# Windowed attention and a token-mixing layer on one core: q in one load per batch with its queries reordered, merged evacuations, cast-in-flight weights, a new order

## The chip, the core and the metric

The kernel runs on 1 core of one Trainium2 chip. The time is the device time of one execution in microseconds (us). The kernel before was run three times, and its median is compared with that of the changed kernel. Engines are called by the names of the profile: PE (TensorE matmul) with PEld (its weight loads), DVE (VectorE), ACT (ScalarE), POOL (GpSimd) and SP (SyncE, which issues stores).

## What is computed

Attention over 576 positions with a causal window of 128 and a distance bias, for 8 batches and 8 heads, and then a layer that mixes the tokens of a batch:

```python
scores = scale * np.matmul(q, k.transpose(0, 1, 3, 2))     # q, k, v: (8, 8, 576, 64)
mask = (rel >= 0) & (rel < 128)                            # rel = query - key
scores = np.where(mask, scores - slopes * abs(rel), -1e9)
attn = exp(scores - max) / sum
x = (attn @ v), heads side by side                         # (8, 576, 512)
wq, wk = x @ w_q, x @ w_k                                  # 512 -> 64
W_tok = (wq @ wk.T) / 8                                    # 576 x 576 for each batch
out = maximum(W_tok @ x, 0) @ w_out                        # float32
```

The kernel takes no maximum, and it evaluates W_tok @ x as wq @ (wk.T @ x): the product G = wk.T @ x is 64 x 512 for a batch.

## The kernel before

Tokens of a batch lie in four blocks of 128 and a tail of 64. Two batches form a pair, and the second layer works on pairs: a batch of a pair has half of the 64-row or 64-column tiles. All work is cut into named steps. `ORDER` (lines 39 to 116) lists every step with its engine (P, D, A, G, S) and, for TensorE, its PSUM bank; each engine runs its steps in this order, and semaphores do the waiting. `:P2` is a whole pair of banks (1024 fp32 columns), `:P21` one bank of pair 2. There are four pairs.

A batch `b` goes through these steps. `g` is a block of keys, `u` half of the heads.

- **Loads.** `Lq`, `Lk` and `Lv` (lines 358 to 381) are GpSimd DMAs that cast fp32 to f16 on the way: one for each block of 128 tokens, with 1024 pieces of 64 elements, and `Lt` for the tails of q and k of a pair. The first blocks of batch 0 come as fp32 through SP and ACT (`LF`). `Lw` and `Lwo` load the weights of the second layer as fp32 through SP, and VectorE casts them (`CWQ`, `CW`).
- **Transposes.** `TQ` (line 495) transposes q and k of one block with eight 128x128 transposes against the identity into one bank; `ETQ` copies the 1024 columns to `qkT`. `TT` and `ETT` do it for the tails, `TF`, `EF`, `TJ`, `EJ` for batch 0.
- **Scores.** `QK` (line 556) multiplies a block of keys with 256 queries, two heads at a time on the two row halves of the array, into a pair of banks. `EXP` (ScalarE) turns 1024 columns into f16 `pt`. `MUL` (VectorE) multiplies `pt` by `bias`, which holds exp of the distance bias and zeros outside the window; it runs once per `u`, and with `biasl` for the last block.
- **Values.** `PV` (line 601) multiplies `pt` by v with a column of ones; `RC` takes the reciprocals of the sums and `X` scales into `x`. `PV b.4` is the tail; it computes 128 rows, of which 64 are used.
- **Second layer.** `XT` and `XTT` transpose x, `EXT` and `EXTT` copy it out; `WQ`, `WK`, `WT` are the projections, `EWQ`, `EWK`, `EWT` their copies; `G` and `EG` make G; `MX` is wq @ G, transposed, in five parts, `RM` and `RMT` the relu to f16 (one instruction for each batch of the pair and each of four column groups, lines 792 to 805); `OUT` is the product with w_out for 128 rows, `EO` copies it to an fp32 buffer and `DO` stores it through SP.

`WM` steps are matmuls on zeros near the start. Two batches are in work at a time, and `OUT` steps of a pair are spread over the attention of the next one. The parameter `mode` says how a step tiles the array: 0 whole, 1 in two row halves, 2 in two column halves, 3 in both; it does not change what is emitted.

## Time and profile before

| | us |
|---|---|
| three runs: median (lowest, highest) | 140.9 (140.62, 145.1) |
| the profiled execution | 141.15 |
| its span | 139.3 |
| PE busy, 1846 matmuls | 125.9 (90%) |
| DVE busy, 254 instructions | 114.1 (82%) |
| ACT busy, 165 instructions | 112.2 (81%) |
| POOL busy, 118 instructions | 95.6 (69%) |
| exp, 64 on ACT, 1.033 each | 62.8 |
| output copies, 35 on ACT, 0.601 each | 20.7 |
| first exp starts, last exp ends | 10.52, 114.87 |
| last load issued on POOL, to landing some 5 later | 102.7 |
| packets of GpSimd's loads | 109,264 |

Busy times are unions over an engine's instructions. Matmuls are pipelined and their ends are modelled, so their duration (379 ns for 512 columns) is longer than the time from one start to the next. The mean granted TensorE clock is 0.987.

### The profile page before, as it was taken

What the parts mean: (1) busy time and instruction counts of PE and PEld (TensorE: products, weight loads), DVE (VectorE), ACT (ScalarE), POOL (GpSimd) and SP (SyncE); (2) the same over time, 40 slices, a digit from 0 to 9 for tenths busy, and PEclk for the clock granted to TensorE, in tenths of its full rate; (3) what the DMA queues carried; (4) which work ended last, traced back from release to release, by engine and by line L of the source; (5) the groups of instructions that cost most, each with busy time, mean ns of one, the idle gap of its engine ahead of it and who ended that gap; (6) DMA issues with size and microseconds to landing.
All of it is one profiled execution on the core that took longest, in us unless ns stands there. A gap on an engine that the chain in (4) does not pass through costs nothing.

```text
span 139.3 us, 4479 instructions
## 1 busy us (share of the span) xinstructions
PE 125.9 (90%) x1846; PEld 84.5 (61%) x1846; DVE 114.1 (82%) x254; ACT 112.2 (81%) x165; POOL 95.6 (69%) x118
## 2 busy tenths in 40 slices
PE   6778599879987999999999999999999999999970
PEld 4445486768744566767866477667765656754420
DVE  5657999999996999999999999999998999705000
ACT  3089969898796999868999999978989995279860
POOL 7999999999919999999999999759940000000000
PEclk9999869999999999999999999999999999999999
DMA  4999999999999999999999999999999975505993
GB/s 103 184 155 154 157 153 153 152 150 177 283 184 156 152 155 152 151 153 150 152 151 154 147 172 270 232 202 152 157 171 272 338 274 216 226 5 171 335 355 121
DMA packets 119332, 25.59 MB, mean 184 GB/s; under 512 B 114192, under 2 KB 114192, under 8 KB 119312
## 3 DMA queue, kind: packets, MB, share of 16 engines
q0 software_dynamic: 109264, 13.77, 155.9%
q1 hardware_dynamic: 8992, 11.28, 24.2%
q10 hardware_dynamic: 1056, 0.26, 0.8%
q8 instruction: 14, 0.23, 0.6%
q14 instruction: 6, 0.05, 0.1%
HBM read 29.62 MB, written 9.44 MB: 280 GB/s over the span
## 4 chain that ended last, share of the span: by engine, by line
PE 58%; POOL 22%; DMA 7%; DVE 7%; issue 2%; ACT 1%; ACTq 0%; POOLq 0%
PE pair L231 47%; POOL nat L363 13%; PE pair L234 11%; DMA natt<-in_k_dram 7%; POOL vt L380 6%; DVE pt L594 3%; DVE qkT L240 2%; POOL natt L370 2%; ACT osb L238 1%; DVE x L634 1%; DVE xT L240 0%; DVE rm L772 0%; POOL wm L298 0%; DVE xTt L240 0%; POOL wm L300 0%
## 5 line engine op out<-in xcount | busy, mean ns | idle before, releaser
L587 ACT ACTIVATE pt<-pair 128x1024 f16<-128x1024 f32 x64 | 62.8, 1033 | 4.0 <-PE pair L231 3.6
L380 POOL DMA_DIRECT2D vt<-in_v_dram x40 | 36.9, 976 | 2.6 <-PE pair L231 2.4
L363 POOL DMA_DIRECT2D nat<-in_k_dram x31 | 30.8, 1036 | 3.5 <-DMA nat<-in_k_dram 3.4
L231 PE MATMUL pair<-wout_sb,rm 128*128 128x512 f16 x128 | 31.6, 379 | 0.0
L594 DVE TENSOR_TENSOR pt<-pt,bias 128x1024 f16<-128x1024 f16 x48 | 31.3, 680 | 0.1
L363 POOL DMA_DIRECT2D nat<-in_q_dram x30 | 30.4, 1039 | 0.3 <-DMA vt<-in_v_dram 0.3
L238 ACT COPY osb<-pair 128x512 f32<-128x512 f32 x35 | 20.7, 601 | 7.4 <-PE pair L231 7.2
L231 PEld LDWEIGHTS <-pt 128*128 128x128 f16 x576 | 21.4, 98 | 8.4 <-issue 2.7
L231 PE MATMUL pair<-vt,pt 128*128 128x65 f16 x576 | 24.1, 195 | 2.3 <-ACT pt L587 1.6
L240 DVE COPY qkT<-pair 128x1024 f16<-128x1024 f16 (+1 forms) x38 | 21.7, 591 | 2.6 <-PE pair L231 1.3
L231 PE MATMUL pair<-qkT 64*128 64x256 f16 (+2 forms) x320 | 21.5, 250 | 1.1 <-DVE x L634 0.5
L634 DVE TENSOR_TENSOR x<-pair,inv 128x512 f16<-128x512 f32 x32 | 21.6, 685 | 0.5
L234 PE MATMUL pair<-identh,nat 128*128 128x128 f16 x244 | 19.3, 226 | 1.4 <-ACT pt L587 0.7
L234 PEld LDWEIGHTS <-nat 128*128 128x128 f16 x244 | 15.2, 101 | 5.8 <-issue 3.6
L231 PEld LDWEIGHTS <-rm 128*128 128x128 f16 x128 | 11.1, 97 | 10.6 <-issue 0.8
L231 PEld LDWEIGHTS <-qkT 64*128 64x128 f16 x320 | 11.3, 94 | 7.7 <-issue 3.2
L770 ACT ACTIVATE rm<-pair 128x512 f16<-128x512 f32 x25 | 13.7, 647 | 0.0
L594 DVE TENSOR_TENSOR pt<-pt,biasl 128x1024 f16<-128x1024 f16 x16 | 10.7, 668 | 0.0
L234 PE MATMUL pair<-identh,x 128*128 128x128 f16 x128 | 9.9, 219 | 0.0
L648 DVE RECIPROCAL inv<-pair 128x8 f32<-128x8 f32 (+1 forms) x40 | 7.8, 200 | 1.2 <-PE pair L231 0.8
L234 PEld LDWEIGHTS <-x 128*128 128x128 f16 x128 | 7.6, 98 | 1.7 <-issue 0.8
L240 DVE COPY xT<-pair 128x1024 f16<-128x1024 f16 x12 | 8.2, 687 | 0.4 <-PE pair L234 0.2
(66 smaller groups left out, 116.7 us busy)
## 6 DMA issues: line engine op xcount, KB each, us to landing
out_dram<-osb SPq DMA_DIRECT2D x32, 256.0 KB, 3.0
vt<-in_v_dram POOLq DMA_DIRECT2D x32, 128.0 KB, 5.5
nat<-in_k_dram POOLq DMA_DIRECT2D x31, 128.0 KB, 5.3
nat<-in_q_dram POOLq DMA_DIRECT2D x30, 128.0 KB, 5.1
osb<-in_moe_w_out_dram SPq DMA_DIRECT2D x4, 256.0 KB, 7.2
out_dram<-osb SPq DMA_DIRECT2D x8, 128.0 KB, 3.9
osb<-in_q_dram SPq DMA_DIRECT2D x4, 128.0 KB, 3.8
natt<-in_q_dram POOLq DMA_DIRECT2D x4, 128.0 KB, 7.1
```

Source lines behind the costliest of these rows:

```text
L231: hold(nc.tensor.matmul(*a, **k))
L234: hold(nc.tensor.transpose(*a))
L238: hold(nc.scalar.copy(out_ap, in_ap))
L240: hold(nc.vector.tensor_copy(out=out_ap, in_=in_ap))
L363: return lambda: nc.gpsimd.dma_start(out=natv(b, j, n), in_=(q, k)[j][b, :, P * n:P * n + P, :].transpose([1, 0, 2]))
L370: nc.gpsimd.dma_start(out=natt_s[pr % 2][:, j].rearrange("p e h d -> p (e h) d"), in_=(q, k)[j][2 * pr:2 * pr + 2, :, 512:576, :].rearrang ...
L380: return lambda: nc.gpsimd.dma_start(out=vtv(b, t)[:n, :, 0:D], in_=v[b, :, P * t:P * t + n, :].transpose([1, 0, 2]))
L587: nc.scalar.activation(out=pt[:, 0:1024], in_=two(s.bank).rearrange("p e c -> p (e c)"), func=AF.Exp, scale=SCALE)
L594: ENG2[o.eng].tensor_tensor(out=pt[:, 0:1024], in0=pt[:, 0:1024], in1=bt, op=ALU.mult)
L634: nc.vector.tensor_tensor(out=x[r].rearrange("p (g h d) -> p g h d", g=2, h=4), in0=sums(p)[r, :, :, 0:64], in1=box["inv"][r].unsqueeze(3) ...
L648: nc.vector.reciprocal(out=box["inv"][r], in_=sums(p)[r, :, :, 64])
L770: hold(nc.scalar.activation(out=out_ap, in_=in_ap, func=AF.Relu, scale=WSCALE))
```

## The change

- q of a whole batch (512 tokens) comes in one load: partition p gets the queries 4p to 4p+3, so a piece is 256 elements instead of 64. Batch 0 loads its second half like this. k keeps one load per block. The tails of q and k go to the two halves of the partitions.
- `TQ` transposes all of q in one step: 32 transposes of 128x64, in column halves. The queries of a block are thereby in another order: position 32r + x holds query 4x + r, in runs of 32. `iota` and `mask` build the bias in this order. x, wq and the mixed rows keep it, until `RM` writes its relu in the order r, x again; `OUT` st then computes the rows 4p + st, and `DO` stores them so.
- The new step `TK` transposes two blocks of k with sixteen pairs of 64x64 transposes in row halves (`tp2`), which write the two banks of a pair. `XT`, `XTT`, `TT` and the k of batch 0 (`TJ`) use `tp2` too and take two banks instead of one.
- `ETQ` copies 2048 columns; `QK` of a batch waits for it. `MUL` runs once for both `u`, 2048 columns, behind both `EXP`; `biasl` goes, the last block takes another slice of `bias`. `RM` does both batches of a pair, or two column groups, in one instruction of 1024 columns.
- The tail's `PV` does two groups of four heads in column halves, one bank, 64 rows each; `RC` and `X` of the tail have 128 partitions and half the columns, and `WT` and `G` take the tail in two halves.
- Weights are loaded by GpSimd with a cast, in four loads; `CWQ`, `CW`, `wz` go.
- The output step (7, 3) is done in two halves of 256 columns, each with its copy and store.
- `NPT` 5 to 6, `NNAT` 4 to 3 (k), `NQ` 2, `OSB` 12 to 14; other `WM` counts. The memsets of the pads of `pt` go.
- `ORDER` is new. At the start `ident` is behind six GpSimd items, and `bias` ahead of the first copies. 13 of 16 `RM` and 33 of 37 `EO` are on ScalarE, three `EO` and each one of `EWK`, `EWQ`, `EG` more than before on VectorE. `LOGB` and its steps are not used, since it is empty.

The diff, cut to what matters here (of the order, its start and its end):

```diff
-NNAT = 4
+NNAT = 3
+NQ = 2
+QR = 4
 NV = 4
-NPT = 5
-PTW = 1088
+NPT = 6
 NX = 4
 
 FIRST32 = ((0, 0), (1, 0), (0, 1))
 
-OSB = 12
-WIDE = ()
-
-WARM = (12, 3, 4, 3, 3, 5,)
+OSB = 14
+
+GROUPS = ((0, 1), (2, 3), (4, 5), (6, 7))
+
+LOGB = ()
+
+LAST = (7, 3)
+
+WARM = (25, 3, 2, 4,)
...
+warm:D LF0.0.1.0:A Lq0.2:G LF0.0.1.1:A LF0.1.0.0:S ones:D iota:G LF0.1.0.1:S LF0.0.0.1:S
+Lk0.1:G wmc:D zeros:D LF0.0.0.0:S mask:G Lk0.2:G bias:A Lq1.0:G ident:G Lk1.0:G idh:D WM.0:P31
+TF0.1.1:P00 pads:D TF0.0.1:P01 EF0.1.1:A Lk1.1:G TF0.1.0:P00 Lt0:G EF0.0.1:A TF0.0.0:P10
+EF0.1.0:A TJ0.1.1:P2 QK0.0.1:P3 EF0.0.0:D TJ0.2.1:P0 EXP0.0.1:A EJ0.1.1:D TJ0.2.0:P10 EJ0.2.1:D
...
+PV7.0:P2 OUT4.2:P11 RC7.2:D RC7.0:D X7.2:D OUT4.1:P00 EO4.2:A X7.0:D EO5.4:D XT7.1:P3 XTT6:P2
+OUT4.0:P11 EXT7.1:D EXTT6:A DO5.4:S EO4.1:A DO4.2:S OUT5.2:P10 DO2.1:S DO4.1:S XT6.1:P0 EO5.2:A
+XT7.0:P3 EXT6.1:D XT6.0:P2 EO4.0:A WT6:P10 EXT6.0:D EXT7.0:A OUT5.1:P11 EWT6:D WK6:P30 EO5.1:A
+DO5.1:S WQ6:P31 EWK6:A DO2.2:S DO3.2:S G6:P30 EWQ6:A DO4.0:S OUT5.3:P31 EG6:D MX6.0:P1 EO5.3:D
+MX6.4:P2 MX6.3:P0 RM6.0:A OUT4.3:P30 RMT6:D DO5.3:S DO2.3:S RM6.3:A MX6.1:P1 EO4.3:D MX6.2:P2
+DO5.2:S OUT7.4:P31 RM6.2:A RM6.1:D DO4.3:S OUT5.0:P30 EO7.4:A OUT7.2:P10 DO7.4:S EO5.0:A
+OUT6.1:P31 DO5.0:S EO7.2:A OUT7.1:P30 DO7.2:S EO6.1:A OUT7.0:P10 DO6.1:S EO7.1:A OUT6.2:P31
+DO7.1:S EO7.0:A OUT6.3:P30 DO7.0:S EO6.2:A OUT6.0:P10 DO6.2:S EO6.3:A OUT7.3b:P31 DO6.3:S
+EO6.0:A OUT7.3a:P30 DO6.0:S EO7.3a:A EO7.3b:A DO7.3a:S DO7.3b:S
...
+    bias = cpool.tile([P, 2, 2, 2, 384], F16, name="bias")
...
+    natq_s = [cpool.tile([P, H, QR, D], F16, name=f"natq{i}") for i in range(NQ)]
+    natk_s = [[cpool.tile([P, H, D], F16, name=f"natk{i}{n}") for n in range(4)] for i in range(NNAT)]
+    natt_s = [cpool.tile([P, 2, H, D], F16, name=f"natt{i}") for i in range(2)]
+    vt_s = [cpool.tile([P, 5, H, VW], F16, name=f"vt{i}") for i in range(NV)]
+    pt_s = [cpool.tile([P, 2, 1024], F16, name=f"pt{i}") for i in range(NPT)]
...
+    def twoh(bank):
+        return pairs[bank[0]].rearrange("p a c -> p (a c)").bitcast(F16).rearrange("p (a c) -> p a c", a=2)
...
+    def tp2(o, m, lo, hi):
+        for r, x in enumerate((lo, hi)):
+            k = slice(64 * r, 64 * r + 64)
+            tp(twoh(o.bank)[:, r, 64 * m:64 * m + 64], x[k], identh[k, k])
...
-        nc.gpsimd.iota(wint, pattern=[[1, 256]], base=0, channel_multiplier=-1)
+        nc.gpsimd.iota(wint[:, 0:256], pattern=[[P, 2], [1, QR], [QR, P // QR]], base=0, channel_multiplier=-1)
+        nc.gpsimd.iota(wint[:, 256:384], pattern=[[-P, 2], [1, 64]], base=P, channel_multiplier=-1)
...
+        keep(0, [[1, QR], [QR, P // QR]], 0, 1)
+        keep(P, [[1, QR], [QR, P // QR]], -1, -1)
+        keep(256, [[1, 64]], -1, -1)
+        keep(320, [[1, 64]], 0, 1)
...
+    def dma_q(b, r0):
+        return lambda: nc.gpsimd.dma_start(
+            out=natq_s[b % NQ][r0 // QR:P].rearrange("p h r d -> p h (r d)"),
+            in_=q[b, :, r0:512, :].rearrange("h (p r) d -> p h (r d)", r=QR))
...
+            wts = [load(("Lw", j, ""), next(i), [lambda j=j, w=w: nc.gpsimd.dma_start(
+                out=wqk_sb[:, :, 64 * j:64 * j + 64], in_=w.rearrange("(c p) j -> p c j", p=P))], 1, [])
+                for j, w in enumerate((moe_w_q, moe_w_k))]
+            wto = [load(("Lwo", c, ""), next(i), [lambda c=c: nc.gpsimd.dma_start(
+                out=wout_sb[:, 2 * c:2 * c + 2, :],
+                in_=moe_w_out[256 * c:256 * c + 256, :].rearrange("(c p) n -> p c n", p=P))], 1, [])
+                for c in range(2)]
...
+        if n == 0:
+            def em(o):
                 for c in range(NHP):
-                    tp(
-                        dst[:, j, c, :],
-                        src[j][:, 2 * c:2 * c + 2, :].rearrange("p a b -> p (a b)"), identh)
-
-        t = add("TQ", b, n, want, pe(0.45), [loads[b, 0, n], loads[b, 1, n], idh], em, banks=1)
-        tq[b, n, 0] = tq[b, n, 1] = [t]
-
-        def ev(o):
-            cp(o.eng, qkT_s[b % 2].rearrange("p j c t -> p (j c) t")[:, :, P * n:P * n + P],
-               oneh(t.bank).rearrange("p (a t) -> p a t", t=P))
-
-        old = [qkd.get((b - 2, g, u)) for g in (n - 1, n) for u in range(2)]
-        evt[b, n] = add("ETQ", b, n, want + 0.6, EV(1.02, 0.69), [t, *old], ev, frees=[t])
+                    for r in range(QR):
+                        for e in range(2):
+                            dst = twoh(o.bank)[64 * e:64 * e + 64, c // 2].rearrange(
+                                "p (c t r x) -> p c r t x", c=2, t=4, r=QR)[:, c % 2, r]
+                            tp(dst, natq_s[b % NQ][:, 2 * c + e, r, :], identh)
+
+            t = add("TQ", b, "", want - 0.2, pe(0.87), [loads[b, 0, 0], idh], em, banks=2, mode=2)
+            tq[b, 2, 0] = [t]
+
+            def ev(o):
+                cp(o.eng, qkT_s[b % 2][:, 0, :, 0:512].rearrange("p (u c) t -> p u c t", u=2),
+                   twoh(t.bank).rearrange("p u (c t) -> p u c t", c=2))
+
+            old = [qkd.get((b - 2, g, u)) for g in range(4) for u in range(2)]
+            evt[b, 0] = evt[b, 1] = add("ETQ", b, "", want + 0.4, EV(1.85, 1.22), [t, *old], ev, frees=[t])
+        if n % 2 == 0:
+            m = n // 2
+
+            def emk(o):
+                for i in range(2):
+                    for c in range(NHP):
+                        x = natk(b, n + i)[:, 2 * c:2 * c + 2, :].rearrange("p a b -> p (a b)")
+                        tp2(o, 2 * c + i, x, x)
+
+            tk = add("TK", b, m, want, pe(0.255), [loads[b, 1, n], loads[b, 1, n + 1], idh], emk,
+                     banks=2, mode=1)
+            tq[b, n, 1] = tq[b, n + 1, 1] = [tk]
+
+            def evk(o):
+                cp(o.eng, qkT_s[b % 2][:, 1, :, 256 * m:256 * m + 256]
+                   .rearrange("p c (n r t) -> p r c n t", n=2, r=2),
+                   twoh(tk.bank)[:, :, 0:512].rearrange("p r (c n t) -> p r c n t", c=4, n=2))
+
+            oldk = [qkd.get((b - 2, g, u)) for g in (n, n + 1) for u in range(2)]
+            evk_[b, m] = add("ETK", b, m, want + 0.6, EV(1.02, 0.69), [tk, *oldk], evk, frees=[tk])
...
+            need = [evt[b, u], evk_[b, g // 2], ett[b] if g == 3 else None]
...
+        bt = bias.rearrange("p u e a (k c) -> p (u e a) k c", c=P)
+        bt = bt[:, :, 0:2, :] if g < 3 else bt[:, :, 0:3:2, :]
+        pv = pt_s[(4 * b + g) % NPT].rearrange("p u (h k c) -> p (u h) k c", k=2, c=P)
 
         def ml(o):
-            ENG2[o.eng].tensor_tensor(out=pt[:, 0:1024], in0=pt[:, 0:1024], in1=bt, op=ALU.mult)
-
-        mul[b, g, u] = add("MUL", b, f"{g}.{u}", w + 1.6, DVE(0.68),
-                           [x, mkb if g < 3 else mkbl], ml)
-
-    ENG2 = {"DVE": nc.vector, "POOL": nc.gpsimd}
+            nc.vector.tensor_tensor(out=pv, in0=pv, in1=bt, op=ALU.mult)
+
+        mul[b, g, 0] = mul[b, g, 1] = add("MUL", b, g, w + 1.6, DVE(1.21), [xs[b, g], x, mkb], ml)
...
+            if qt == 4:
+                px = one(o.bank)
+                for h in range(4):
+                    for i, kb in enumerate((3, 4)):
+                        for g in range(2):
+                            mm(px[64 * g:64 * g + 64, 65 * h:65 * h + 65], ptc(kb, 4 * g + h, kb == 4, 64),
+                               vtv(b, kb)[:, 4 * g + h, 0:65], start=(i == 0), stop=(i == 1))
+                return
...
+                    x = x_s[b % NX][2 * i + n][:, P * c:P * c + P]
+                    tp2(o, 2 * c + n, x, x)
+
+        t = add("XT", b, i, want, pe(0.45), [xop[b, 2 * i], xop[b, 2 * i + 1]], em, banks=2, mode=1)
...
+            def ev(o):
+                relu(o.eng, rm_s[pr % 2][:, db].rearrange("p r e (t x) -> p (e t) r x", t=4),
+                     two(t.bank).rearrange("p e (t r x) -> p (e t) r x", t=4, r=QR))
+
+            rm = add("RM", bs[0], db, want + 0.4, EV(1.05, 1.2), [t, *old], ev, frees=[t])
             for e in range(2):
...
+    def rows_of(b, r):
+        return out[b, 0:512, :].rearrange("(p r) c -> r p c", r=QR)[r]
...
+        for h in range(2):
+            cs = slice(256 * h, 256 * h + 256)
+
+            def em(o, cs=cs):
+                for db in range(4):
+                    mm(one(o.bank)[:, 0:256], rm_s[pr % 2][:, db, st, SIDE[b], :],
+                       wout_sb[:, db, cs], start=(db == 0), stop=(db == 3))
+
+            t = add("OUT", b, f"{st}{'ab'[h]}", want, pe(0.43), need, em, banks=1)
+            osd[b, st] = t
+            box = {}
+
+            def ev(o, t=t, box=box):
+                box["o"] = spool.tile([P, DM], FP32, name="osb", tag="osb", bufs=OSB)
+                cp(o.eng, box["o"][:, 0:256], one(t.bank)[:, 0:256])
+
+            e = add("EO", b, f"{st}{'ab'[h]}", want + 1.1, EV(0.4, 0.42), [t], ev, frees=[t])
+
+            def dm(o, cs=cs, box=box):
+                nc.sync.dma_start(out=rows_of(b, st)[:, cs], in_=box["o"][:, 0:256])
+
+            add("DO", b, f"{st}{'ab'[h]}", want + 1.8, {"SP": (0.7, 2.5)}, [e], dm)
```

609 lines of the change are left out of this document (307 added, 302 removed).

## The prediction

> **What bounds the kernel now.** I read the busy slices first, then a table of stretches that I cut at the first and the last exp (10.52 and 114.87 us) and at the last x (120.2), then waits, groups and the TensorE timeline. The profiled execution took 141.15 us: a span of 139.3 and 1.85 around it; the median of the runs is 140.9.
>
> ```profile
> PE   6778599879987999999999999999999999999970
> DVE  5657999999996999999999999999998999705000
> ACT  3089969898796999868999999978989995279860
> POOL 7999999999919999999999999759940000000000
> ```
>
> No engine carries it alone: from slice 5 to 34 VectorE is at 9 but for two slices, ScalarE mostly at 8 or 9, TensorE at 9 from slice 14 on (a slice is 3.48 us).
>
> ```profile
> 10.52:43.70 33.18, 27.22 (x469) 20.86 (x465) 30.29 (x67) 27.98 (x32) 29.78 (x36) 0.95 2.21 173
> 43.70:77.00 33.30, 33.15 (x534) 23.07 (x534) 32.88 (x66) 31.01 (x47) 33.30 (x40) 1.00 2.38 152
> 77.00:108.00 31.00, 30.98 (x486) 20.67 (x486) 29.84 (x59) 28.36 (x41) 22.78 (x27) 1.00 2.09 198
> 108.00:114.87 6.87, 6.87 (x111) 4.28 (x111) 6.53 (x14) 6.56 (x11) 0.00 (x0) 1.00 0.84 306
> 114.87:120.20 5.33, 5.33 (x80) 3.71 (x78) 5.09 (x11) 2.60 (x6) 0.00 (x0) 1.00 0.52 199
> 120.20:139.30 19.10, 14.69 (x127) 7.00 (x124) 3.12 (x6) 11.38 (x24) 0.00 (x0) 0.99 0.58 206
> ```
>
> Columns: stretch, length, then busy time of TensorE, its weight loads, VectorE, ScalarE, GpSimd; granted clock; DMA. From the first exp to the last x VectorE is busy 104.6 of 109.7 us (95.4%). From the first to the last exp ScalarE is busy 93.9 of 104.35, idle 10.4. TensorE looks full, but its ends are modelled, so I count it by starts. Behind the last PV (its end is near 118.8 us) TensorE hardly pauses until 134.95, and 4.35 us of copy and store follow. GpSimd's waits are small (3.4 us for a load, 2.4 for PV).
>
> ```profile
> 110.16 0.61 PE L234 MATMUL pair<-identh,x 128*128 128x128 f16 x8
> 110.71 0.29 PE L231 MATMUL pair<-wqT,gs 64*128 64x64 f16 x8
> 110.83 0.60 PE L231 MATMUL pair<-qkT 64*128 64x192 f16 x12
> ...
> 122.31 0.32 PE L231 MATMUL pair<-xTt,wqk_sb 128*64 128x64 f16 x8
> 122.46 1.03 PE L231 MATMUL pair<-xT,wqk_sb 128*64 128x512 f16 x8
> ```
>
> Starts give the pace: eight 64x64 row-tiled matmuls take 0.12 us, eight column-tiled ones of 64 columns 0.15, eight full transposes 0.45 when the next is full too (64.23 to 64.68) and 0.55 here, so a change of tiling costs 0.10.
>
> ```profile
> L594 DVE TENSOR_TENSOR pt<-pt,bias 128x1024 f16<-128x1024 f16 x48 | 31.3, 680 | 0.1
> L240 DVE COPY qkT<-pair 128x1024 f16<-128x1024 f16 x25 | 16.8, 681 | 0.4 <-PE pair L234 0.2
> L770 ACT ACTIVATE rm<-pair 128x512 f16<-128x512 f32 x25 | 13.7, 647 | 0.0
> L240 DVE COPY qkT<-pair 128x512 f16<-128x512 f16 x13 | 5.1, 418 | 2.1 <-PE pair L231 1.3 <-PE pair L234 0.6
> ```
>
> From 512 to 1024 columns a copy grows by 0.263 us: 0.155 is fixed. That prices the merged instructions.
>
> **TensorE.** By starts the old order is 104.1 us of matmuls and 95 changes of tiling (9.5). q and k of blocks: 28 groups at 0.45 and 5 at 0.22 (13.7). New: k in 14 groups of sixteen 64x64 transposes at 2 x 0.12 = 0.24, and 3 at 0.12; q in 7 groups of 32 half-width ones, and one half. No row has that shape. Unpaired it is 32 x 0.056 = 1.8, at the pace of the 64-column row 32 x 0.019 = 0.6; I take 16 pairs x 0.056 = 0.90, because WQ's eight 512-column matmuls take 0.87 and so do run in pairs. Sum 10.5: -3.2. XT 16 x (0.45 - 0.24): -3.4. TT 4 x (0.46 - 0.24): -0.9. XTT: -0.4. PV of the tail, 8 x (0.48 - 0.30): -1.4. WT: +0.7. Eight more changes of tiling: +0.8. Together -7.8; were no row pairs concurrent, +0.9.
>
> **VectorE.** Merged products: 2 x 0.68 against 0.68 + 2 x 0.263 = 1.21 (bounds 1.16 and 1.36), 32 times: -4.8, less 1.5 because adjacent ones already start 0.62 apart: -3.3. Tail x 128x256 instead of 64x512: 8 x 0.26 = -2.1. q and k copies: 25 x 0.68 against 6 x 1.21 + 11 x 0.68: -2.3. ETT and EXTT that go to ScalarE -1.2, first copies -1.0, biasl -2.0, weight casts -2.0, memsets -0.5, merged relus -0.9. Taken over from ScalarE: three output copies +2.1, EWK, EWQ, EG +2.1, two EWT +1.3, one RMT +0.7. Sum -9.1: 114.1 becomes 105.0. But 7.4 now stand behind the last x instead of 3.1, so up to it 111.0 becomes 97.6.
>
> **ScalarE.** The total stays at 112: relus 13 x 1.03 for 25 x 0.55 (between EXT's 1.02 and 2 x 0.65), copies -1.4, casts and RMT -3.6, but bias +0.8, q, k and tail copies +3.5, first copies +1.0. What counts is between the first and the last exp. Out of there go 3 output copies (1.8), 19 relus against 8 merged ones (4.0), 2 RMT, 2 casts, 1 EWT, 1 EXT (4.1); q, k and tail copies add 3.1. Scaled by 0.95 for overlap: -6.5, from 93.9 to 87.4.
>
> **Loads.** 22 issues fewer of q at 0.87 us from start to start, four weight issues more (two of 512 pieces, two of 256, some 1.5 us). 109,264 packets are 109 issues with 16 extra each; the new list gives 87,500. On GpSimd's queue the loads of q now wait for the transposes two batches back, of k three back, and later loads queue behind them; its queue gets 17 us shorter, so I price this at nothing. Without that cover each such wait costs up to its length (the one at 38 us was 3.4). SyncE loses the five weight loads and waits at the head of its queue for nothing else; it only stores, and the stores are not on the path before the end.
>
> **Start.** Identity moves behind six items of GpSimd: about 6.3 us instead of 1.31. Bias (2.56, now 3 x 128 columns, 3.4) moves ahead of the first copies, into the 3.9 us in which ScalarE waited; it ended 0.4 us before the first exp. First exp 9.5 instead of 10.52 (bounds 8.5 and 11.5).
>
> **Tail.** Behind the last PV TensorE now has 14.6 us of output matmuls (18 instead of 12, one halved), 5.4 of the rest and 11 changes of tiling: 21.1 (16.2 before, with 0.4 idle). With 0.4 idle and 4.1 for the end (the halved last copy saves 0.25): 25.6.
>
> **Sum.** ScalarE sets the middle: 9.5 + 87.4 + 10.4 idle = 107.3 for the last exp, product and PV 2.0, tail 25.6: 134.9. VectorE would allow its last x at 9.5 + 92.6/0.954 = 106.6, and the last PV some 2 us earlier, so the idle time that it and TensorE caused on ScalarE should shrink; with half of it gone the span is 129.7. I take 2.6 us of it: 132.3. With 1.85 around it, less 0.25 between this execution and the median: 134 us. The case's own range is 131 to 137.
>
> **Rivals.** (a) Loads set the pace. They end 17 us earlier and all follows: 139.3 - 17 + 1.6 = 124 us. For it: DMA busy throughout. Against it: GpSimd waits for PV near the end, and VectorE has no gaps in which it waits for data. 4%.
>
> (b) PSUM, slower. TQ, TK, XT, TT and XTT, 45 groups, now take a whole pair of banks where they took one: 394 banks are handed out instead of 361, out of 4 pairs, of which an exp holds one for 1.03 us. If each waits a quarter of an exp in line on TensorE, 45 x 0.26 = 11.7 us, the span is 132.3 + 11.7 = 144, 145.6 us. It decides from 0.15 us each. For it: TensorE waited for ScalarE's pt 2.3 us in four places. Against: with less work TensorE comes earlier to such waits without ending later. 9%. The Trainium skill says the same in TensorEngine Tiling (Array Packing), Restrictions and Gotchas: different row tiles write to different PSUM banks. Every QK here takes such a pair.
>
> (c) Longer chains eat the gain. A merged product waits for both exps, with copies and x queued behind it on VectorE, so PV comes 0.94 us later; QK of a batch waits for all of q, 0.9 + 1.21 to 1.85 instead of 0.45 + 0.68. If TensorE and ScalarE lose 1 us at each of 7 batches, the span is 139.3: 140.9 us. Against: two batches are interleaved. 9%.
>
> (d) The tiled transposes do not do what they are for: pairs run one after another, TensorE is at +0.9 instead of -7.8, and the time stays at 139 to 142. The 64x64 row speaks against it. 4%. The Trainium skill, same page, Performance Considerations, says that column tiling disables the fast weight load. If the column-tiled loads then stood unhidden at the 0.11 us of the 128*64 weight rows, q would cost 7 x (32 x 0.11 - 0.9) = 18 us more; the eight in 0.15 us, with their loads, show no such thing.
>
> **Numbers.** A difference under 2% (below 138.1 or above 143.7 us is outside) cannot be told from none. My forecast has 74%. Faster: it and (a), 78%. Within: (c) and (d), 13%. Slower: (b), 9%. The range reaches from a first exp at 8.5 with two thirds of the idle time gone (134.9 - 1.0 - 6.9 + 1.6 = 128.6) to about half of (c) and (d) (139.5), and leaves out (a), (b) and the rest of those: about 2 in 10.
>
> **What would show it.** Right: sixteen 64x64 transposes start 0.24 us apart, the merged product near 1.2 us, ScalarE busy about 87 us between first and last exp, the last exp near 105, 25 us behind the last PV. Wrong: matmuls waiting for pt or x at the two-bank transposes (b), exps waiting for QK at each new batch (c), TK at 0.45 (d), or a first exp after 11.5.

## The result, and the profile after

| | before | after |
|---|---|---|
| median of four (lowest, highest), us | 140.81 (140.62, 145.1) | 144.83 (144.31, 145.42) |
| ratio to before, 95% interval | | 1.0291 [1.024, 1.0342] |
| profiled execution, its span | 141.15, 139.3 | 144.91, 143.1 |
| TensorE busy, matmuls | 125.9, 1846 | 123.6, 2314 |
| VectorE, ScalarE busy | 114.1, 112.2 | 107.1, 112.3 |
| packets of GpSimd's loads | 109,264 | 87,472 |

The forecast was 134 us, faster; the changed kernel is slower by 2.9%. Ratios, here and below, leave out executions that lie over 1.5% above the fastest of their kernel; medians are of all. The busy slices of the changed kernel (a slice is 3.58 us; they are counted from 0 here):

```profile
PE   7599758888599899996999989997999989999960
...
DVE  4227999899477999996999999879998985555000
ACT  0877999989807998977899999787999935748660
POOL 6899996999499979598989897100000000000000
PEclk9968999999959999999999999999999999999997
```

Two dents stand in the middle, where the kernel before has a shallow one at most (its slice 12: PE 7, DVE 6): slices 10 and 11 on all three engines (PE 5 and 9, DVE 4 and 7, ACT 8 and 0, with the granted clock at 5 in slice 11), and slice 18 (PE 6, DVE 6, ACT 8). Cut at the first and last exp, at the last PV and around these two places (stretch, length, busy time of TensorE, its weight loads, VectorE, ScalarE, GpSimd; granted clock; DMA):

```profile
11.39:36.97 25.58, 20.78 (x557) 16.00 (x551) 23.93 (x43) 24.50 (x26) 23.59 (x29) 1.00 2.20 163
36.97:43.90 6.93, 5.23 (x70) 3.04 (x70) 3.26 (x6) 2.68 (x5) 5.20 (x7) 0.75 2.00 174
43.90:66.30 22.40, 21.54 (x449) 13.75 (x441) 21.38 (x34) 20.24 (x25) 19.54 (x24) 1.00 2.18 165
66.30:68.60 2.30, 1.04 (x24) 0.70 (x22) 1.02 (x3) 0.72 (x5) 1.90 (x3) 1.00 2.46 154
68.60:112.79 44.19, 41.32 (x868) 27.10 (x866) 41.32 (x70) 41.36 (x52) 19.33 (x23) 1.00 1.45 160
11.39:112.79 101.40, 89.90 (x1951) 60.59 (x1947) 90.92 (x152) 89.50 (x109) 69.55 (x83) 0.98 1.86 163
112.79:116.98 4.19, 3.79 (x82) 2.67 (x81) 3.56 (x8) 2.82 (x5) 0.00 (x0) 1.00 0.61 192
116.98:143.10 26.12, 21.33 (x241) 10.69 (x238) 8.72 (x17) 14.16 (x23) 0.00 (x0) 0.96 0.66 223
```

Against the forecast's sum (9.5 to the first exp, 95.2 to the end of the last, 2.0 to the last PV, 25.6 behind it: 132.3), the four stretches are 1.9, 6.2, 2.2 and 0.5 us longer. In 36.97 to 43.90 ScalarE works 2.68 of 6.93 us. The timeline of TensorE shows what it does at the two places (start, length, line, operation; in brackets the idle time before it and what ended it):

```profile
36.33 0.64 PE L234 MATMUL pair<-wqk_sb,xT 128*128 128x64 f16 x16
...
38.67 0.95 PE L234 MATMUL pair<-wqk_sb,xT 128*128 128x64 f16 x16 [1.71 <-issue]
...
66.00 0.39 PE L234 MATMUL pair<-vt,pt 128*128 128x65 f16 x7
...
67.64 0.45 PE L234 MATMUL pair<-vt,pt 128*128 128x65 f16 x9 [1.26 <-issue]
```

Both pauses fall inside one step (the 32 matmuls of WK0, the 16 of PV3.3), between matmuls that need nothing from another engine. "issue" means that the profile shows nothing that was waited for. From 38.82 to 42.23 the granted clock is half, so the 6.93 us cost more than the pause.

The page's queue table names one thing that grew, the loads of instructions. Before and after:

```profile
q8 instruction: 14, 0.23, 0.6%
...
q8 instruction: 18, 0.29, 0.8%
```

The columns are packets, MB and share; a load is 16 KB. Counting the recorded TensorE instructions (a weight load and a matmul each), one such load belongs to every 256. I set beside each other when TensorE passes a boundary of 256, when the next load starts, when it has landed, and when TensorE gets to the next boundary (the count misses some records, so the boundaries are good to a few tenths):

```
kernel   boundary passed   load starts after   landed   next boundary reached   idle there
before   90.2              3.8                 94.91    97.6                    -
after    32.2              4.0                 37.12    36.97                   1.71
after    61.7              3.5                 66.10    66.39                   1.26
after    104.3             0.2                 105.49   113.1                   -
```

Both pauses end 1.5 us after a landing (38.67 and 67.64), some 2.5 after the start of that load. While GpSimd's loads run, a load of instructions mostly starts 1.8 to 5.7 us after the boundary in the changed kernel and its variants (0.2 to 4.5 in kernels with the old order); when they are over, mostly within 1. In the kernel before, 256 instructions last 6.2 us or more, and the delay is hidden. In the changed kernel the dense places (64-wide transposes in pairs, WT, WK) run through 256 in 4.5 to 4.7. The Trainium skill, Runtime: NRT & Kernel Launch, Instruction fetch mechanics, gives the same 256 instructions in 16 KiB and says that crossing costs one DMA step, "mostly hidden". The trace agrees on the size and, here, not on the rest: 1.71 and 1.26 us.

### The profile page after: what moved, and what is told of

It is laid out like the page before. It is cut to its first block, busy times and chain, and to the rows that moved or that the text cites. A ratio compares the mean times of both kernels' runs of the same rounds, so it can differ in the third digit from the quotient of the medians.

```text
span 143.1 us, 5331 instructions
## 1 busy us (share of the span) xinstructions
PE 123.6 (86%) x2314; PEld 79.9 (56%) x2314; DVE 107.1 (75%) x193; ACT 112.3 (78%) x147; POOL 79.3 (55%) x103
## 3 DMA queue, kind: packets, MB, share of 16 engines
q0 software_dynamic: 87472, 14.42, 133.2%
## 4 chain that ended last, share of the span: by engine, by line
PE 59%; DVE 18%; ACT 15%; issue 5%; ACTq 0%; DVEq 0%
PE pair L234 50%; PE pair L237 9%; ACT pt L638 5%; DVE x L714 5%; DVE qkT L248 4%; DVE pt L653 4%; ACT bias L343 2%; ACT rm L859 2%; ACT xT L246 1%; DVE xT L248 1%; ACT qkT L246 1%; DVE inv L704 1%; DVE xtl L708 1%; ACT L343 1%; DVE vt L328 1%
## 5 line engine op out<-in xcount | busy, mean ns | idle before, releaser
L653 DVE TENSOR_TENSOR pt<-pt,bias 128x2048 f16<-128x2048 f16 x32 | 38.6, 1213 | 0.7 <-ACT pt L638 0.7
L234 PE MATMUL pair<-wout_sb,rm 128*128 128x512 f16 (+1 forms) x132 | 31.2, 373 | 0.4 <-DVE xtl L708 0.3
L375 POOL DMA_DIRECT2D natk<-in_k_dram x31 | 27.8, 908 | 4.3 <-DMA natq<-in_q_dram 2.2
L246 ACT COPY osb<-pair 128x512 f32<-128x512 f32 (+1 forms) x33 | 18.6, 578 | 7.6 <-PE pair L234 6.6
L234 PE MATMUL pair<-vt,pt 128*128 128x65 f16 (+1 forms) x576 | 21.9, 194 | 2.3 <-issue 1.3
L234 PEld LDWEIGHTS <-pt 128*128 128x128 f16 (+1 forms) x576 | 18.7, 100 | 8.0 <-issue 4.7
L248 DVE COPY qkT<-pair 128x1024 f16<-128x1024 f16 (+2 forms) x28 | 19.4, 704 | 1.8 <-PE pair L237 1.6
L859 ACT ACTIVATE rm<-pair 128x1024 f16<-128x1024 f32 x13 | 12.9, 1037 | 2.4 <-PE pair L234 2.4
L237 PE MATMUL pair<-identh,natq 128*64 128x128 f16 (+1 forms) x256 | 8.3, 217 | 0.4 <-ACT qkT L246 0.4
L237 PEld LDWEIGHTS <-natq 128*64 128x64 f16 (+1 forms) x256 | 7.3, 110 | 1.6 <-issue 0.7
```

Of the source, the lines that this page charges most:

```text
L234: hold(nc.tensor.matmul(*a, **k))
L237: hold(nc.tensor.transpose(*a))
L246: hold(nc.scalar.copy(out_ap, in_ap))
L248: hold(nc.vector.tensor_copy(out=out_ap, in_=in_ap))
L375: return lambda: nc.gpsimd.dma_start(out=natk(b, n), in_=k[b, :, P * n:P * n + P, :].transpose([1, 0, 2]))
L653: nc.vector.tensor_tensor(out=pv, in0=pv, in1=bt, op=ALU.mult)
```

## The experiments

Medians are compared by their ratio to the kernel before on the same chip; the changed kernel's is 1.0291, and 1% is 1.4 us.

**1. Moving the boundaries.** The first group of warming matmuls, 25 of 256 columns, becomes 121 of 16 or 57 of 128, so that all later TensorE instructions sit 192 or 64 places further on in their blocks. The group takes 3.40 or 4.93 us instead of 4.66; the transposes behind it start at 7.31 us as before.

```diff
-            for _ in range(n):
-                mm(one(o.bank)[:, 0:256], warm[:, 0:P], warm, ...)
+            w = 16 if i == 0 else 256        # second kernel: 57 of 128 columns
+            for _ in range(121 if i == 0 else n):
+                mm(one(o.bank)[:, 0:w], warm[:, 0:P], warm[:, 0:w], ...)
```

> The changed kernel, only that the first group of warm-up matmuls is 121 of 16 columns instead of 25 of 256, which pushes every later TensorE instruction back by 192 places in its code (a code block is 256 instructions: 18 loads of 16 KB each on the instruction queue for some 4,600 instructions). Code theory: TensorE ran dry at 37.0 us for 1.7 us and at 66.4 for 1.3 because 256 instructions ran faster (4.5 us) than a block came (3.5 to 4 us in line behind GpSimd's loads and 2.2 to arrive); cutting the unstalled trace 192 places earlier leaves 0.7 us of such deficit instead of 3.7. Expected: both pauses and the half clock at 39 us gone or under 0.5 us, ScalarE's wait of 4.0 us for G under 1, 139 to 141.5 us. Bank theory (two-bank transposes wait for pairs) and chain theory (merged products and whole q come late): nothing that they name changes, 144 to 145.5 us.

> The same with 57 warm-up matmuls of 128 columns: code pushed back by 64 places. Code theory: the deficit by the same cut is 5.7 us instead of 3.7, so the pauses stay, at other places, and the time is 144 to 148 us, at least 2 us above the shift by 192. Bank and chain theories: as before the shift, 144 to 145.5 us, and the same as the shift by 192.

Measured: 192 instructions, median 144.62 (142.88 to 144.91), ratio 1.0229 [1.0162, 1.0297]; 64 instructions, median 144.17 (141.77 to 144.95), ratio 1.0111 [1.0073, 1.0149] from the four shortest of nine executions. The code theory misses its numbers: the first shift was to gain 3 us or more, and the second to come out at least 2 us above the first. By the medians the 144 to 145.5 us of the other two theories fit both. The traces tell more. In the profiled execution of the first (142.88) the pause at 66 is gone, and that at 37 has become a shorter one in another step, G0:

```profile
40.72 0.41 PE L234 MATMUL pair<-xtl,wkt 128*64 128x256 f16 x4 [1.03 <-issue]
```

From 11.58 to 141.28 its clock is 1.0, and its exps run 1.86 us ahead of the changed kernel's from 45 us on and 2.9 from 68 on. Its other executions are 1.6 to 2.0 us longer, and they have no trace. The profiled execution of the second (144.63) has three pauses over 1 us, 1.03, 1.02 and 1.41.

What the pauses share is their place in the count. In the traces of the changed kernel and of its variants with all loads (these two and the ones below), TensorE stands behind "issue" for over 0.2 us 25 times between 14 and 115 us (16 times for 0.89 us or more). Each time the matmul that follows has the place 187, 188 or 189 in its 256 of the recorded TensorE instructions, counted from 0, whatever step stands there. In the traces with light loads (experiment 4) and in those of the old order there is no such stop. So the pauses move with the position of the code and belong to the boundaries, but a shift alone only deals them anew: the dense places are too many.

**2. Fewer instructions.** `TK`, and `XT` of the first six batches, as whole 128x128 transposes: 416 TensorE instructions fewer.

```diff
-                        tp2(o, 2 * c + i, x, x)
+                        tp(twoh(o.bank)[:, c // 2, 256 * (c % 2) + P * i:256 * (c % 2) + P * i + P], x, identh)
```

> The changed kernel with TK, and XT of batches 0 to 5, as full 128x128 transposes (half the matmuls), each still in two banks and with the same order: 416 TensorE instructions fewer, some 5.5 us more of TensorE streaming, spread over 26 steps. Code theory: blocks last longer than they take to come, no pause over 0.5 us between 15 and 100 us, 139.5 to 143 us. Bank and chain theories: the pairs are still taken and the chains are as long, and TensorE has more to do: 145 to 150 us.

Measured: 144.45, ratio 1.0214 [1.0154, 1.0274], between the two expectations. No stop behind "issue" over 0.2 us between 15 and 100 us is left, and 16 loads of instructions. But the groups show the price (before the bar: busy time, mean ns):

```profile
L237 PE MATMUL pair<-identh,natk 128*128 128x128 f16 x112 | 8.6, 219 | 0.7 <-DMA vt<-in_v_dram 0.3 <-DVE qkT L248 0.2
...
L237 PE MATMUL pair<-identh,x 128*128 128x128 f16 x96 | 7.2, 220 | 0.5 <-DVE x L714 0.5
```

TensorE's busy time goes from 123.6 to 129.0. The row pairs had saved what was predicted; undoing them trades the pauses for matmuls, and the time nearly stays. Matmuls are not all of it: this execution's granted clock is half from 9.79 to 16.62 (8.10 to 11.51 in the changed kernel), and its exps are 1.9 us late by 16 us.

**3. An earlier start.** Identity first on GpSimd, and the exp's table loaded early.

> The changed kernel with the identity built first on GpSimd, as before, and one exp of one column on ScalarE behind its first loads, so that the activation table is loaded (1.28 us) while ScalarE waits for the mask. My start term was 1.9 us too small: expected first exp at 9.0 to 9.8 us instead of 11.39. If the start is carried to the end: 142.5 to 143.5 us; if later waits eat it: 144 to 145 us. The code blocks keep their places in the code, so the two pauses should stay.

Measured: 146.63, ratio 1.0397. The timeline:

```profile
8.71 2.44 PE L238 MATMUL pair<-ident,osb 128*128 128x128 f32 x10 [2.21 <-DMA osb<-in_q_dram]
```

With the identity there at 1.3 us ten of the twelve transposes wait for the first fp32 blocks of q instead, which land at 8.7; the first exp comes at 11.94, not earlier than 11.39. The pause at 37 is down to 0.31 us, though the code kept its places, that at 66 stays, and one of 2.17 us up to 99.70, with a half clock from 100.91 to 104.33, makes the rest.

**4. Fewer bytes behind which instructions wait.** From batch 3 (q) or 4 (k, v) on GpSimd loads two of eight heads; all other instructions stay.

```diff
-            out=natk(b, n), in_=k[b, :, P * n:P * n + P, :].transpose([1, 0, 2]))
+            out=natk(b, n)[:, 0:HL(b, 4)], in_=k[b, 0:HL(b, 4), P * n:P * n + P, :].transpose([1, 0, 2]))
```

> This kernel leaves out three quarters of GpSimd's loads of the later batches: from batch 3 (q) and 4 (k, v) on only two of the eight heads are loaded, and the rest of each buffer keeps older values. Same order, same instructions on every other engine, about 36,000 packets fewer. Theory (TensorE pauses because the loads of its instructions are late behind GpSimd's packets): the blocks of instructions start under 1.5 us behind the boundary from about 45 us on instead of 2 to 5.6, the pause of 1.5 us at 66 and the one of 1.05 at 97.7 are gone, the one at 37 stays, and the time is 142.0 to 143.5 us, 1.3 to 2.8 less than the changed kernel's 144.8. Rival (loads of data set the pace): VectorE and TensorE no longer wait for v, k and q at all and the time falls by more than 5 us, below 139.8. Rival (the pauses hide other waits that end no earlier): under 0.7 us, 144.1 or more.

and its control, the same in the kernel before:

> The kernel before with three quarters of GpSimd's later loads left out: two of eight heads, for q and k from batch 5 and for v from batch 4 on. It is the control of the light loads in the changed kernel. The kernel before has no pause of TensorE between 16 and 118 us that ends with the landing of instructions, so if the light loads helped the changed kernel by way of its instructions, the time here changes by less than 0.7 us (140.2 to 141.5). If they helped by way of data that comes earlier, or by less traffic in general, it falls here by 2 us or more, too.

Measured: 140.98, ratio 0.9965 [0.9933, 0.9996], 4.6 us less than the changed kernel by the ratios; the control, with 77,008 packets instead of 109,264, 141.03, ratio 0.9997 [0.9967, 1.0028]. In the changed kernel, now with 57,520 packets, the loads of instructions start at most 0.9 us after the boundary from 52 us on, and both pauses are gone. Its WK0, and its windows:

```profile
36.23 1.23 PE L234 MATMUL pair<-wqk_sb,xT 128*128 128x64 f16 x32
```

```profile
11.39:107.89 96.50, 87.95 (x1949) 59.91 (x1945) 90.55 (x152) 89.53 (x109) 62.95 (x83) 1.00 1.28 117
107.89:112.07 4.18, 3.78 (x82) 2.66 (x81) 3.55 (x8) 2.81 (x5) 0.00 (x0) 1.00 0.62 192
112.07:138.10 26.03, 21.33 (x241) 10.68 (x238) 8.71 (x17) 14.18 (x23) 0.00 (x0) 0.99 0.66 224
```

All 32 matmuls of WK0 run in one piece, the stretch between the exps is 4.90 us shorter, and the other two are the same to 0.1. Set against the changed kernel exp by exp, 3.4 us come at the first pause and 1.4 at the second, 0.1 elsewhere. That speaks against earlier data; the control, which has as much less traffic and no pauses, does not move. That the pauses are late instructions is shown: 5.0 us of the profiled span. The 5.0 is one execution against one. The first pause, 3.4 of it, is down to 0.31 and 0.26 us in the profiled executions of experiments 3 and 6, too, whose loads are whole (that load of instructions started 2.8 and 2.4 us after its boundary there, 4.0 in the changed kernel); the 4.6 of the ratios is the firmer figure. The expectation had 1.3 to 2.8, since it kept the first pause. It also counted a pause near 97.7; that stop stays as long as it was (0.78 us, behind VectorE's copies of `qkT`), so it was none. Without them the kernel takes as long as the one before, so the rest of the expected gain went elsewhere.

**5. Which engine sets the middle.** Useless work of like length on one engine at a time, first in the changed kernel, then where TensorE has no pauses to absorb it.

```diff
+            if u == 0 and g % 2 == 0:            # ScalarE, behind 16 exps
+                nc.scalar.copy(junk[:, 0:320], ...)
+            if g % 2 == 0:                       # VectorE, behind 16 products
+                nc.vector.tensor_tensor(out=junk, in0=bf, in1=bf, op=ALU.mult)
+            mm(px[:, 0, 0:512], warm[:, 0:P], ..., start=True, stop=True)   # TensorE, ahead of 32 PV
```

> Adds sixteen copies of 320 columns to ScalarE, one behind each first exp of key blocks 0 and 2, whose results nobody uses; some 0.41 us each, 6.6 us in all, between the first and the last exp. If ScalarE sets the middle, as the prediction has it, the time grows by nearly all of it: 5.5 to 7 us, to 150.3 to 151.8. If ScalarE follows TensorE or VectorE and has room, the copies fall partly into its 12 us of idle time and the time grows by less than 4 us, below 148.8.

> Adds sixteen products of 512 columns to VectorE, one behind each merged product of key blocks 0 and 2, whose results nobody uses; 0.42 us each, 6.7 us in all. If ScalarE sets the middle, VectorE has 10 us of room there and the time grows by less than 3 us, below 147.8. If VectorE is as much the bound as ScalarE, it grows by 5 to 7 us, to 149.8 to 151.8.

> Adds one matmul of 512 columns on zeros ahead of each of the 32 whole-array value products, in the bank that the product then overwrites; 0.21 us each at the full clock, 6.8 us in all, and only 64 more TensorE instructions. If ScalarE sets the middle and TensorE has room since the change, the time grows by less than 3 us, below 147.8. If TensorE is the bound in the middle in spite of its smaller work, it grows by 5 to 7 us, to 149.8 to 151.8.

> The light loads (two of eight heads from batch 3 or 4 on) with 32 more matmuls of 512 columns on zeros, one ahead of each whole-array value product, 0.21 us each, 6.8 us in all. Against the light loads alone (141.0), where TensorE has no pauses to absorb it. If TensorE still sets the middle: 5 to 7 us more, 146 to 148. If ScalarE sets it, as the prediction had it: under 2.5 us more, below 143.5.

> The light loads with sixteen more copies of 320 columns on ScalarE, 0.47 us each, some 0.36 from start to start, 5.8 us in all. If ScalarE sets the middle: 4.5 to 6 us more, 145.5 to 147. If it follows the others: under 2.5 us more, below 143.5.

> The light loads with sixteen more products of 512 columns on VectorE, 0.42 us each, 5.4 to 6.7 us in all. If VectorE sets the middle: 4.5 to 6.5 us more, 145.5 to 147.5. If it follows: under 2.5 us more, below 143.5. If all three engines share the bound, each of the three additions costs about half of its length, 2.5 to 4 us.

> The kernel before with the same 32 matmuls of 512 columns, 6.8 us. If TensorE was the bound before and the change has relieved it, the time grows here by more than with the light loads in the changed kernel, by 5 to 7 us, to 146 to 148; if the share is the same in both, taking 7.8 us of work from TensorE can't have been worth more than that share of it, in either order.

Measured medians and ratios to before:

| added | length | changed kernel | with light loads | us by the ratios, light |
|---|---|---|---|---|
| nothing | | 144.83, 1.0291 | 140.98, 0.9965 | |
| ScalarE | 5.7 | 145.83, 1.0331 | 143.82, 1.0154 | 2.7 |
| VectorE | 6.7 | 146.65, 1.0372 | 144.86, 1.0243 | 3.9 |
| TensorE | 6.8 | 148.27, 1.0470 | 145.38, 1.0245 | 3.9 |
| TensorE, kernel before | 6.8 | | 145.78, 1.0303 | 4.3 |

(The length is sixteen times 0.468 less 0.11 of overlap, sixteen times 0.417, and 32 times 0.213.) In the changed kernel the pauses swallow most of ScalarE's addition: its exps are 3.0 us late at 38 us and level again behind the first pause. Without pauses each engine passes on about half, ScalarE the least. The intervals reach 1.2 to 1.7 us to each side, so the order of the three isn't settled; that none passes on all of its addition is. Each of the three traces with light loads and an addition has one more 3.41 us of half clock (between 19.8 and 26.1) than the trace without; what it costs is in these figures. In the changed kernel the additions cost 0.6, 1.1 and 2.5 us by the ratios, all within what their expectations call room, but the pauses hide what they are worth. Of the expectations for the light loads, the one in which the three engines share the bound is met; neither of the others is met for any engine. TensorE's share was about the same before (0.63 against 0.58); its 4.3 us miss the 5 to 7 of a TensorE that was the bound.

**6. The merged product undone.**

```diff
-            nc.vector.tensor_tensor(out=pv, in0=pv, in1=bt, op=ALU.mult)
+            for x in (first, 1 - first):
+                s = slice(4 * x, 4 * x + 4)
+                nc.vector.tensor_tensor(out=pv[:, s], in0=pv[:, s], in1=bt[:, s], op=ALU.mult)
```

> The changed kernel with each merged product of bias and exp undone: two instructions of 1024 columns in the same place, the first for the half whose exp comes first; 0.15 us more of VectorE for each of 32, 4.8 us in all. If the merged product's wait for both exps is a cost that came with the change (rival c of the prediction), the time falls by 1 us or more, below 143.8. If VectorE's work there is what counts, the time grows by its share as measured with the added products (1.8 of 6.7 us): 1 to 1.5 us, to 145.8 to 146.4.

Measured: 145.05, ratio 1.0297 [1.0236, 1.0359]: no difference. Both numbers of the expectation were missed. The edit changes two things at once, an earlier first half and more work for VectorE (busy 108.9 us instead of 107.1; 4.8 more had been counted), which can cancel; its trace also has 0.26 us in place of the pause at 37, and half clock from 18.82 to 25.64. So it shows that undoing the merged product gains nothing, not that the wait for both exps costs nothing.

**7. A start rebuilt.** iota, identity and mask ahead of GpSimd's loads, `bias` ahead of the copies, the first copies on VectorE, the first QK behind two transposes.

> Another start, the rest of the order as in the changed kernel: iota, identity and mask run on GpSimd ahead of its loads, the table of the exp is loaded early, ScalarE does bias ahead of everything else, the first copies go to VectorE, and the first QK stands behind the two transposes that it needs instead of behind all of them. First exp at 7 to 8.5 us instead of 11.4. If the start adds to the time as the prediction summed it, the time falls by as much as the first exp comes earlier, 2.5 to 4 us, to 141 to 142.3. If what follows waits for its loads, the loads, which now start 1 to 2 us later, take it back: by the exp of batch 2 the gain is under 1 us, and the time is 143.8 or more.

Measured: 147.93, ratio 1.0491. ScalarE's timeline:

```profile
7.66 1.02 ACT L641 ACTIVATE pt<-pair 128x1024 f16<-128x1024 f32 x1 [0.98 <-PE pair L235]
9.98 1.02 ACT L641 ACTIVATE pt<-pair 128x1024 f16<-128x1024 f32 x1 [1.29 <-PE pair L235]
12.94 1.94 ACT L641 ACTIVATE pt<-pair 128x1024 f16<-128x1024 f32 x2 [1.94 <-PE pair L235]
```

The first exp comes 3.7 us earlier, and by the fifth the kernel is 0.6 behind. Not for the loads, as I had expected: the first copies now line up on VectorE, TensorE stops three times (1.1 us from one matmul's start to the next), and from 12.07 to 15.49 its clock is half, so that the 32 transposes of TQ1 take 1.92 us instead of 1.08. Pauses of 1.61, 1.16 and 1.54 us, up to 66.13, 80.17 and 100.23, do the rest.

**8. Parts of the change in the old order.** Weights by GpSimd with a cast; with it the halved last output; with both the tail's PV in column halves (with its x, WT and G).

```diff
-            wts = add("CWQ", "", "", -1.1, EV(0.59, 0.4), [lw], ...)
+            wts = [load(("Lw", j, ""), next(i), [lambda j=j, w=w: nc.gpsimd.dma_start(...)], 1, []) ...]
...
-DO6.3:S EO7.1:A DO7.1:S
+DO6.3:S EO7.1a:A DO7.1a:S EO7.1b:A DO7.1b:S
...
-                    mm(px[:, h // 4, 65 * (h % 4):65 * (h % 4) + 65], ptc(kb, h, cur), ...)
+                    mm(px[64 * g:64 * g + 64, 65 * h:65 * h + 65], ptc(kb, 4 * g + h, kb == 4), ...)
```

> Only the weights through GpSimd with a cast, in the kernel before and its order. Tells the two parts of the other run apart: 139.5 to 140.2 us if VectorE's 2.0 us count by 0.58, 140.6 to 141.1 if they stood in idle time.

> Two parts of the change alone, in the kernel before and its order: the weights of the second layer come through GpSimd with a cast in four loads (the five casts on VectorE, 2.0 us, go), and the last output step, (7, 1) there, is done in two halves of 256 columns. No TensorE work changes but for four more matmuls of half the width. If VectorE shares the bound by the 0.58 that the added products showed, the casts are worth 1.2 us and the halves 0.25: 139.2 to 140 us against 140.9. If the casts stood in idle time of VectorE (it waits near 41 us, where the weights are first used), only the halves count: 140.5 to 140.9.

> A third part of the change alone, in the kernel before and its order, on top of the weights by cast and the halved last output: the tail's value products do two groups of four heads in column halves of the array, one bank instead of a pair, and the tail's x is 128 partitions by 256 columns instead of 64 by 512; WT and G take the tail in two halves; XTT stays whole. VectorE loses 8 x 0.26 = 2.1 us, TensorE 1.4 less some 0.6 for WT and eight changes of tiling. By the shares that the additions showed (0.58 of VectorE's time, 0.65 of TensorE's): 1.2 us of VectorE and nothing to 0.5 of TensorE, 138.2 to 139.0 against 140.0. If the longer WT and the changes of tiling outweigh it, 139.8 or more.

Measured: weights alone 140.26, ratio 0.9922 [0.9883, 0.996]; with the halves 139.97, 0.9896 [0.9849, 0.9943], the fastest kernel of the study; with the tail too 141.15, 0.9982 [0.9945, 1.002]. The casts and the halves are worth 1.1 and 0.4 us, near the 1.2 and 0.25 expected; the 0.4 alone lies inside the intervals. The tail's tiling gives them back: VectorE's busy time falls from 112.1 to 110.3, nearly the 2.1 counted, but TensorE's grows from 126.1 to 127.1 with 56 more matmuls, where 0.7 less had been predicted. Part of the growth is the clock, which is half from 17.73 to 21.14 in this execution and whole there in the other; from 22 us on the distances between matmul starts under 0.3 us add up to 99.8 against 99.3. So the saving is missing either way. Which of the two extra costs took it, the longer WT or the changes of tiling, wasn't tried.

## Why the prediction was wrong

**The step that failed: "so I price this at nothing".** The step on loads looked at packets, at GpSimd's queue and at waits for data. Its count was right (87,472 packets against 87,500), and TensorE waits for no data in the middle. But its instructions are loaded, too, behind GpSimd's loads, and the change made them 25% more (2,314 matmuls against 1,846) in places that are denser. 5.0 of the 10.8 us by which the span was missed are the two pauses and the half clock behind the first one (shown by the light loads and their control). The trace of before had the rows: 14 instruction loads with delays up to 4.3 us. I priced tiled transposes by their starts alone, never by their number. The other 5.8 us are terms of the sum that were too small, as the span with light loads shows (138.1 against 132.3): the start 1.9, product and PV 2.2, the stretch between the exps 1.3, the tail 0.4. The pauses made the kernel slower; without them it would still have missed the forecast, at the time of the kernel before.

**TensorE -7.8: right, and worth half.** The distances between matmul starts that are under 0.3 us add up, from 10.7 us on, to 105.6 us before and 97.5 after: -8.1. The tiled k transposes took 0.24, q 1.0 with its change of tiling, as counted. But waits of 0.35 us and more went from 20 with 11.3 us to 37 with 21.0, and without the pauses there are still 30 with 15.4. So of 8.1 us saved, some 4 came back as short waits.

**VectorE -9.1, ScalarE the same in sum: right within 2.1.** VectorE fell by 7.0, ScalarE stayed:

```profile
L653 DVE TENSOR_TENSOR pt<-pt,bias 128x2048 f16<-128x2048 f16 x32 | 38.6, 1213 | 0.7 <-ACT pt L638 0.7
...
L859 ACT ACTIVATE rm<-pair 128x1024 f16<-128x1024 f32 x13 | 12.9, 1037 | 2.4 <-PE pair L234 2.4
```

1.21 and 1.03 had been predicted. Between the exps ScalarE was to be busy 87.4 and was 89.5. Its durations fell by 5.9 (105.6 to 99.7; 6.8 were listed), and their union only by 4.4: I had scaled by 0.95, while the union is 0.89 of the sum before and 0.90 after.

**"ScalarE sets the middle": the size near, the reason not.** Without the pauses ScalarE's idle time there is 7.0 us (7.8 predicted) and the stretch 96.5 (95.2). Yet an addition on ScalarE costs about half of its length, and the other two pass on about as much. No one engine sets the middle; a sum along one of them hits by what it assumes of its idle time, so the near hit here is luck in part.

**First exp at 9.5: it was 11.39.**

```profile
3.99 1.28 ACT L343 ACT_TABLE_LOAD   x1 [3.99 <-DVE wm L324]
...
5.29 3.41 ACT L343 ACTIVATE bias<-wm 128x384 f16<-128x384 f32 x8
...
7.31 3.28 PE L237 MATMUL pair<-ident,osb 128*128 128x128 f32 x12 [1.60 <-POOL ident masks.py:199]
```

I had left out that the table load stands behind bias's wait for wm, which shifts bias and the copies behind it, and that the twelve transposes, all behind the late identity, take 3.28 us (0.41 each, 0.29 in the kernel before). From 8.10 to 11.51 the granted clock is half, where the kernel before has it whole, and the QK ahead of the first exp takes 0.62 us for its four matmuls instead of 0.39; how much of the 1.9 us is the clock wasn't tried. And the term was no term of a sum: the rebuilt start had its first exp at 7.66 and ended later.

**Product and PV 2.0: it was 4.19, and 3.90 before.**

```profile
112.28 1.22 DVE L861 TENSOR_SCALAR rm<-pair 128x1024 f16<-128x1024 f32 x1
...
113.41 1.22 DVE L653 TENSOR_TENSOR pt<-pt,bias 128x2048 f16<-128x2048 f16 x1
...
114.37 1.03 PE L234 MATMUL pair<-wout_sb,rmt 128*128 128x512 f16 x4
...
116.24 0.90 PE L234 MATMUL pair<-vt,pt 128*128 128x65 f16 x24 [0.37 <-DVE x L714]
```

I added one product and one PV. In the order a merged relu stands ahead of the last product on VectorE (0.6 us behind the exp's end), an output step stands between the PVs, and then a PV waits for x to give up its banks. The prediction itself has the last PV of before near 118.8 us, 3.9 behind the last exp: better than my sum.

**Tail 25.6: right, 26.1.** It is where most of the gain went that was left: 5.6 us more than before (20.5), because six more output steps stand behind the last PV, where TensorE's time counts in full. The stretch between the exps did shrink, by 7.85 us without the pauses.

**The rivals.** (a) Loads set the pace: no, the control doesn't move. (b) PSUM, the one that had the sign: no, TensorE waited for ScalarE's pt 1.8 us in four places, 2.3 before; the waits are in the page's list:

```profile
PE pair L234 <- issue: 3.0, 2, 1.7
PE pair L234 <- ACT pt L638: 1.8, 4, 0.8
```

(c) Longer chains: undoing the merged product gains nothing, which doesn't price its wait alone, and the QK that wait for all of q were not tried; open. (d) Transposes that don't pair: no, sixteen take 0.24 us. (The Trainium skill, TensorEngine Tiling (Array Packing), has the sentence on the fast weight load under Restrictions and Gotchas, not under Performance Considerations; the 32 half-width transposes of q take 1.0 us, so the trace shows no such cost.) The rival that happened was not on the list.

## What to carry to other kernels

A change that makes matmuls smaller and more numerous must be priced by instructions per microsecond too: find how long 256 TensorE instructions last at the densest place, and compare it with the delay and the landing of an instruction load in the trace (here mostly 1.8 to 5.7 us plus 2.5), while the other loads run. Where three engines are each some 90% busy, work on one is worth about half of its length (here 0.47 to 0.63 for what was added, 1.1 of 2.0 us for the casts taken away; the tail's tiling gave nothing), and a term for the start is worth nothing until what follows it is shown to come earlier. Where the trace of before has the stretch itself, its length is a better start for the sum than two durations out of it.

## What the runs showed of the hardware

- Loads of instructions are late while GpSimd's loads run: mostly 1.8 to 5.7 us from boundary to start in the changed kernel's order, mostly under 1 us when those are light or over.
- A pause of 1.71 us was enough for a half clock of 3.41 us (38.82 to 42.23); the one of 1.26 at 66.4 was not. Length alone doesn't decide: in the rebuilt start a pause of 1.61 us (to 66.13) was not followed by one, and one of 1.54 (to 100.23) was, from 100.82 on. The Trainium skill, TensorE: Matmul & The Clock Gate, has windows of 3413 ns and the lower clock after an idle one; the length agrees, but no 3.4 us of idle time was needed here.
- Executions of the same program spread by 1.1 us (144.31 to 145.42) to 3.2 (141.77 to 144.95 with a shift of 64 instructions). The kernel before, without such pauses, spreads too (140.52 to 142.58 in 17 executions), so the spread is not put down to them.
